# Weight splits issued one group of products earlier, and two edits in the first tile, in an attention and channel-mixing kernel

## The chip, the core and the metric

The kernel runs on one core of a Trainium2 chip. The metric is device time of the core in microseconds (us), the median of several runs. Five engines run at once, each with its own queue of instructions in order: PE (TensorE, matrix products), DVE (VectorE), ACT (ScalarE), POOL (GpSimd) and SP (SyncE, which issues most of the DMAs). An instruction of one engine that needs another's result waits in its queue, and all that stands behind it waits too.

## What is computed

Reference, cut to what matters (8 batches, 8 heads, 576 tokens, head size 64, 32 packed tokens, model width 512):

```
p_packed = softmax_attention(p, k, v)                    # 32 queries over 576 keys
attn     = softmax_attention(q, p_packed, p_packed)      # 576 queries over 32 keys
x  = attn as (batch, 576, 512)
u  = x + real(fft(fft(x, axis=tokens), axis=channels))
un = (u - mean(u)) / sqrt(var(u) + 1e-6)                 # over the 512 channels
out = u + relu(un @ w_ch1) @ w_ch2                       # w_ch1 512x2048, w_ch2 2048x512
```

## The kernel before

The 4608 tokens of the output form 36 blocks of 128, and four blocks form a tile: nine tiles, called 0 to 8 here. For each tile `ffn` (L650) runs the two layers of the channel mixing over 16 chunks `j` of 128 hidden units. A product in full precision is made of three products of rounded parts, high by high, high by low and low by high, so every operand is split into a high and a low part: `split` (L96) is a copy on ACT (L97, the high part) and a subtraction (L98, the low part), on POOL where it is told so.

- `up(j)` (L658) makes 12 products with the four 128-column pieces of w1's chunk `j` into the PSUM bank `ph` (L669); then ACT applies relu into `hh` (L672) and DVE makes the low part `hl` (L673). `ph` is one bank in all tiles but the last two, so `up(j+1)` can't start before `hl` of `j` has read it.
- `down(j)` (L676) makes 12 products of `hh`, `hl` with w2's chunk `j` into four banks `acc` (L683). It is issued one chunk late: the order on PE is `up(j)`, `down(j-1)`, `up(j+1)`, `down(j)`.
- The weights are split anew in every tile: `wsplits` (L640) is a generator that splits one chunk of w1 or w2 at each `next(splits)`, in the order w1 0, w1 1, w2 0, w1 2, w2 1, w1 3 and so on. The parts `wr_h` and `wr_l` live in a ring of six buffers, three chunks. A chunk's split takes the place of the chunk three earlier: that of w1 `j+1` waits until `down(j-2)` is over, that of w2 `j` until `up(j)` is.
- `step(i)` (L763) is called twice for each `j` (32 steps a tile): after `up(j)` and after `down(j-1)`. It issues one stage of `front(t+1)` (L235), the attention and the spectrum of the next batch, whose stages `ORDER` (L40) lists; steps 0 and 2 issue what is left of the batch before.

Stages of the front that are spoken of: scores of the packed queries and their exponentials (L263, L288), their transposes (L297, L300), the second scores (L263, `s2T`, with `s2Tt` in the bank `ph`), their transposes on DVE (L368), subtraction of maximum, mean and division (L374 to L419), the transpose to `a` (L421), `folded` (L424: sums and differences of token pairs, L431 to L436), `folded_rest` (L439: ten small ones, L449 to L462), `folded_parts` (L468: `fh`, `xl`, `ol`, `fl`), and the blocks of the result `u` (L554 to L578). `EF` (L32) says by batch and group of heads which engine folds: 0 is DVE, 1 is POOL.

In tile 0 the weights also come in. They arrive as 64-bit floats; a chunk is fetched by SP (`fetch`, L145), ACT makes two halves of it (`halves_of`, L167 and L168) and DVE joins these to the 32-bit chunk that stays in SBUF (`joined`, L172). `step(i)` of tile 0 joins a chunk, fetches the chunk three later into the place that this frees (three places, two of them tagged `wst`, one in `ubuf`), issues the front's stage and then halves the next chunk.

Inside a tile the order on PE, DVE, ACT and POOL is the order of the code (`manual_schedule`, L782). Ahead of tile 0, and where tile 0 begins, a scheduler sets the order.

Of the kernel before, what the change touches and what calls it, by code (L numbers as in the profile page):

```python
# [28 lines left out]
EN = ((0, 1), (1, 0), (0, 0))  # L29


EF = (((0, 0, 0, 0), (1, 1, 0, 0)), ((1, 1, 1, 1), (0, 0, 0, 0)), ((0, 0, 0, 0), (0, 0, 0, 0)))  # L32
ES = (1, 0, 0)
EO = (0, 0, 0)

# [40 lines left out]
def tile_kernel(ctx, tc, kpT, qT, v, w1, w2, tabs, tabR, tabB, tabT, sel, ident_d, out):  # L76
# [68 lines left out]
    def fetch(j, n):  # L145
        i = stages.pop(0)
        if i is None:
            st = work.tile([P, 512, 2], I32, tag="wst", name="wst", bufs=2)
        elif i < 0:
            st = spot(n, i, [P, 512, 2]).bitcast(I32)  # L150
        else:
            st = ubuf[:, i:i + 2, :].rearrange("p a n -> p (a n)").bitcast(I32).rearrange("p (n t) -> p n t", t=2)
        nc.sync.dma_start(st, (w1, w2)[n][:, j, :].bitcast(I32).rearrange("p (n t) -> p n t", t=2))
        fetched[j, n] = st
# [8 lines left out]
    def halves_of(j, n):  # L163

        st, high, c = words(j, n)
        fifth = st.rearrange("p n t -> p (n t)").bitcast(U8).rearrange("p (n t) -> p n t", t=8)[:, :, 3]
        nc.scalar.activation(c.bitcast(F32), high.bitcast(F32), AF.Prelu, scale=REBIAS, alpha=SIGN)  # L167
        nc.scalar.activation(high, fifth, AF.Copy, scale=1.0 / 32, bias=-31.0 / 64)  # L168

    def joined(j, n):  # L170
        st, high, c = words(j, n)
        nc.vector.scalar_tensor_tensor(c, c, 3, high, ALU.logical_shift_left, ALU.bitwise_or)  # L172
        del fetched[j, n]
# [25 lines left out]
    def next_step():  # L199
        steps[0] = (steps[0] or 0) + 1  # L200
        for item in [x for x in due if x[0] <= steps[0]]:
            due.remove(item)
            item[1]()
# [31 lines left out]
    def front(b):  # L235
# [188 lines left out]
        def folded(g):  # L424
# [4 lines left out]
            ec, oc = eo[:, 0, :], eo[:, 1, :]  # L429
            e1, e2, e3, e4 = [(nc.vector, nc.gpsimd)[i] for i in EF[min(b, 2)][g]]  # L430
            e1.tensor_tensor(ec[:, 0:287], a[:, 0:287], a[:, NE:S], ALU.add)  # L431
# [208 lines left out]
    def wsplits():  # L640

        for _ in tiles:
            for n, j in [(0, 0)] + [x for j in range(1, NJ) for x in ((0, j), (1, j - 1))] + [(1, NJ - 1)]:
                hi = work.tile([P, DM], F32R, tag="wr", name="wr_h", bufs=6)
                lo = work.tile([P, DM], F32R, tag="wr", name="wr_l", bufs=6)
                split(hi, lo, (w1f, w2f)[n][:, j, :], nc.gpsimd)
                ready.append((hi, lo))
                yield

    def ffn(first, turned, step, nxt, alone, following):  # L650
        keys = turned.keys
        n = len(keys)
        T = n * P
        uh, ul = turned.hl
        acc = [psf.tile([P, DM], F32, tag=f"acc{i}", name=f"acc{i}") for i in range(n)]
        now["acc"] = acc

        def up(j):  # L658
            wh, wl = ready.pop(0)

            pool, tag = (ps, "ps") if alone and j % 2 else (psf, "ph")
            ph = pool.tile([P, 512], F32, tag=tag, name="ph")

            step = T // 2 if first == 0 and j < SPL else T
            order = sorted(range(12), key=lambda k: k % 3 == 1) if j == 0 else range(12)
            for t in (slice(i, i + step) for i in range(0, T, step)):
                for n, k in enumerate(order):
                    c, (l, r) = k // 3, ((wh, uh), (wh, ul), (wl, uh))[k % 3]
                    nc.tensor.matmul(ph[:, t], l[:, c * P:(c + 1) * P], r[:, c, t], start=(n == 0), stop=(n == 11))  # L669
            hh = work.tile([P, 512], F32R, tag="hh", name="hh")  # L670
            hl = work.tile([P, 512], F32R, tag="hl", name="hl")
            nc.scalar.activation(hh[:, :T], ph[:, :T], AF.Relu)  # L672
            nc.vector.scalar_tensor_tensor(hl[:, :T], ph[:, :T], 0.0, hh[:, :T].bitcast(F32), ALU.max, ALU.subtract)  # L673
            return hh, hl

        def down(j, hh, hl, moves=()):  # L676

            moves = list(moves)
            vh, vl = ready.pop(0)
            for i in range(n):  # L680
                w = slice(i * P, (i + 1) * P)
                for k, (l, r) in enumerate(((hh, vh), (hh, vl), (hl, vh))):
                    nc.tensor.matmul(acc[i], l[:, w], r, start=(j == 0 and k == 0), stop=(j == NJ - 1 and k == 2))  # L683
                    if moves:
                        moves.pop(0)()

        kinds = [nxt.kind(h, following) for h in range(2)] if nxt else []
        assert kinds in ([], ["new", "late"], ["old", "new"], ["old", "old"]), kinds

        prev = None  # L690
        late = "late" in kinds
        for j in range(NJ):
            last = nxt is not None and j == NJ - 1
            cur = up(j)
            next(splits, None)
            if last:
                next(splits, None)
                nxt.parts(0)
                nxt.parts(1)
            step(2 * j)  # L700
            if j == 11:
                for h in range(2):
                    if kinds[h:h + 1] == ["old"]:
                        nxt.less_quarters(h)
                        nxt.turn(h)
            if prev is not None:
                down(j - 1, *prev, nxt.moves(2) + [lambda: None] * 4 + nxt.moves(3) if last and late else ())
                if j == 13:
                    for h in range(2):
                        if kinds[h:h + 1] == ["new"]:  # L710
                            nxt.less_quarters(h)
                if last:
                    nxt.parts(2)
                    nxt.parts(3)
                else:
                    next(splits, None)
                if late and j == NJ - 2:
                    nxt.less(2, True)
                    nxt.less(3, True)
            step(2 * j + 1)  # L720
            if j == 13:
                for h in range(2):
                    if kinds[h:h + 1] == ["new"]:
                        nxt.turn(h)
            prev = cur
        down(NJ - 1, *prev)
        next(splits, None)
        for i, key in enumerate(keys):
            u = u_of[key]
            nc.vector.scalar_tensor_tensor(u, acc[i], stat_of[key][:, 2:3], u, ALU.mult, ALU.add)  # L730
            nc.sync.dma_start(out[(first + i) * P:(first + i + 1) * P, :], u)
            free.append(place_of[key])
# [19 lines left out]
    rest = gen0  # L752
    for j in range(ORDER[0].count("D"), LEAD):
        load_weights(j)
    ready, splits = [], wsplits()
    next(splits)
    next(splits)
    for t, (first, tk) in enumerate(tiles):

        gen = front(t + 1) if t + 1 < B else iter(())  # L760
        ended = []

        def step(i):  # L763

            next_step()

            k = i + 2 * LEAD
            if t == 0 and i > 0 and k <= 2 * NJ:
                joined((k - 1) // 2, (k - 1) % 2)
                if 8 < k + 2 < 2 * NJ:  # L770
                    fetch((k + 2) // 2, (k + 2) % 2)
            if i in (0, 2):
                next(rest, None)
            elif not ended and next(gen, None) == "rest":
                ended.append(gen)
            if t == 0 and k < 2 * NJ:
                halves_of(k // 2, k % 2)
            assert i < 2 * NJ - 1 or t + 1 >= B or ended

        nxt = Turned(tiles[t + 1][1]) if t + 1 < len(tiles) else None  # L780

        with tc.manual_schedule(engines=MANUAL):  # L782
            ffn(first, cur, step, nxt, t + 1 >= B, t + 1)
        cur, rest = nxt, gen
# [112 lines left out]
```

## Time and profile before

| | us |
|---|---|
| median of 3 runs | 1008.71 (1008.37 to 1009.35) |
| the profiled execution | 1006.72 |
| its span, first to last instruction | 1004.90 |
| PE busy in the span | 953.4 (95%) |
| DVE, ACT, POOL busy | 585.5, 463.1, 477.4 |

The span falls in three: the front of batch 0 until 61 us, where PE mostly waits; tile 0 from 61 to 184 us; and eight more tiles of 91 to 107 us each. A row with a number in square brackets tells how long its engine stood idle before it, and what ended that wait.

### The profile page before, as it was taken

The page shows a single profiled execution, that of the slowest core. Times are in us where ns is not written, and L with a number is a line of the kernel's source. Part 1 is how long each engine was busy: PE and PEld are TensorE (multiplying, and loading weights), DVE is VectorE, ACT ScalarE, POOL GpSimd, SP SyncE. Part 2 cuts the span into 40 slices and gives each one's busy share as a digit, 9 for nine tenths or more (in the row PEclk, how much of TensorE's full clock was granted, in tenths as well). Part 3 has the DMA queues.
Part 4 walks back from the last instruction along what each step waited for, and adds up shares of the span by engine and source line. Part 5 has one row for each costly group of instructions (what it writes and reads, how often), then busy time and mean ns, then how long its engine had stood idle before and what let it go on. Part 6 is the DMA issues. An engine that isn't in the chain of part 4 may idle for free.

```text
span 1004.9 us, 14998 instructions
## 1 busy us (share of the span) xinstructions
PE 953.4 (95%) x5588; PEld 782.7 (78%) x5588; DVE 585.5 (58%) x1221; ACT 463.1 (46%) x942; POOL 477.4 (48%) x426
## 2 busy tenths in 40 slices
PE   4188999999999999999999999999999999999998
PEld 2176778778887888788877888788878888888886
DVE  4767795559455855578466946595658562123112
ACT  4456775544453445435544445444534453343322
POOL 3714663364345444454455434643555354545443
PEclk9599999999999999999999999999999999999999
DMA  9216442320042002300240013101410010011001
GB/s 359 110 47 201 147 147 78 130 73 0 2 133 81 0 2 73 115 1 10 58 167 1 1 56 132 48 1 47 141 48 1 22 64 1 1 28 57 0 1 42
DMA packets 28169, 65.93 MB, mean 66 GB/s; under 512 B 5494, under 2 KB 12992, under 8 KB 28096
## 3 DMA queue, kind: packets, MB, share of 16 engines
q1 hardware_dynamic: 27120, 63.53, 19.3%
q0 software_dynamic: 976, 1.44, 0.5%
q8 instruction: 44, 0.72, 0.3%
q14 instruction: 29, 0.24, 0.1%
HBM read 48.70 MB, written 9.44 MB: 58 GB/s over the span
## 4 chain that ended last, share of the span: by engine, by line
PE 79%; DVE 8%; issue 5%; POOL 4%; ACT 3%; DMA 0%; POOLq 0%; DVEq 0%; ACTq 0%
PE ph L669 34%; PE acc L683 32%; POOL wr_l L98 2%; DVE turned L413 1%; DVE turned L409 1%; PE po L320 1%; DVE w2f L172 1%; PE s L263 1%; PE px L231 1%; PE py L231 1%; PE px L233 1%; PE px L232 1%; PE py L232 1%; PE py L233 1%; ACT hh L672 1%
## 5 line engine op out<-in xcount | busy, mean ns | idle before, releaser
L98 POOL TENSOR_TENSOR wr_l<-w1f,wr_h 128x512 fp32r<-128x512 f32 x144 | 192.8, 1339 | 367.6 <-ACT wr_h L97 367.3
L673 DVE SCALAR_TENSOR_TENSOR hl<-ph,hh 128x512 fp32r<-128x512 f32 x144 | 98.9, 687 | 322.5 <-ACT hh L672 322.0
L98 POOL TENSOR_TENSOR wr_l<-w2f,wr_h 128x512 fp32r<-128x512 f32 x144 | 196.4, 1364 | 90.5 <-ACT wr_h L97 88.4
L669 PE MATMUL ph<-uh,wr_h 128*128 128x512 f32 (+1 forms) x580 | 228.4, 394 | 4.1 <-DVE s L368 2.5
L683 PE MATMUL acc<-wr_l,hh 128*128 128x512 f32 x576 | 226.5, 393 | 2.6 <-POOL wr_l L98 2.5
L669 PE MATMUL ph<-uh,wr_l 128*128 128x512 f32 (+1 forms) x580 | 225.7, 390 | 1.7 <-POOL wr_l L98 1.7
L683 PE MATMUL acc<-wr_h,hh 128*128 128x512 f32 x576 | 226.6, 393 | 0.0
L683 PE MATMUL acc<-wr_h,hl 128*128 128x512 f32 x576 | 225.8, 392 | 0.0
L672 ACT ACTIVATE hh<-ph 128x512 fp32r<-128x512 f32 x144 | 86.1, 598 | 295.3 <-PE ph L669 295.1
L669 PE MATMUL ph<-ul,wr_h 128*128 128x512 f32 (+1 forms) x580 | 220.5, 389 | 1.1 <-DVE stat L207 1.1
L669 PEld LDWEIGHTS ph<-uh,wr_h 128*128 128x128 f32 x580 | 109.1, 188 | 37.8 <-issue 8.1
L669 PEld LDWEIGHTS ph<-uh,wr_l 128*128 128x128 f32 x580 | 109.0, 188 | 25.7 <-POOL wr_l L98 2.5
L683 PEld LDWEIGHTS acc<-wr_l,hh 128*128 128x128 f32 x576 | 108.4, 188 | 26.1 <-POOL wr_l L98 4.7
L683 PEld LDWEIGHTS acc<-wr_h,hl 128*128 128x128 f32 x576 | 108.4, 188 | 23.0
L669 PEld LDWEIGHTS ph<-ul,wr_h 128*128 128x128 f32 x580 | 108.8, 188 | 22.2 <-DVE stat L207 1.3
L683 PEld LDWEIGHTS acc<-wr_h,hh 128*128 128x128 f32 x576 | 108.3, 188 | 22.2
L97 ACT CAST wr_h<-w2f 128x512 fp32r<-128x512 f32 x144 | 88.9, 617 | 0.0
L97 ACT CAST wr_h<-w1f 128x512 fp32r<-128x512 f32 x144 | 88.3, 613 | 0.0
L231 PE MATMUL py<-gh,fh 128*128 128x258 f32 x64 | 19.3, 301 | 26.8 <-ACT fh L473 26.8
L211 ACT ACTIVATE junk<-ubuf,stat 128x512 f32<-128x512 f32 x36 | 25.7, 716 | 27.1 <-DVE stat L207 27.1
L98 POOL TENSOR_TENSOR gl<-turned,gh 128x516 fp32r<-128x516 f32 x16 | 24.9, 1555 | 24.6 <-ACT gh L97 24.6
L231 PEld LDWEIGHTS py<-gh,fh 128*128 128x128 f32 x64 | 12.9, 202 | 27.9 <-ACT fh L473 27.4
(202 smaller groups left out, 1299.4 us busy)
## 6 DMA issues: line engine op xcount, KB each, us to landing
kp<-kpT SPq DMA_DIRECT2D x16, 608.0 KB, 3.9
out<-ubuf SPq DMA_DIRECT2D x36, 256.0 KB, 2.1
vt<-v SPq DMA_DIRECT2D x14, 640.0 KB, 5.0
wst<-w SPq DMA_DIRECT2D x17, 512.0 KB, 3.6
qt<-qT SPq DMA_DIRECT2D x14, 576.0 KB, 4.4
raw<-flip SPq DMA_DIRECT2D x208, 32.0 KB, 1.8
ubuf<-w SPq DMA_DIRECT2D x9, 512.0 KB, 3.7
w1f<-w SPq DMA_DIRECT2D x3, 512.0 KB, 13.6
```

The source lines that it names most:

```text
L97: nc.scalar.copy(hi, src)
L98: (lo_eng or nc.vector).tensor_tensor(lo, src, hi.bitcast(F32), ALU.subtract)
L172: nc.vector.scalar_tensor_tensor(c, c, 3, high, ALU.logical_shift_left, ALU.bitwise_or)
L211: nc.scalar.activation(junk, u, AF.Square, bias=st[:, 1:2], scale=1.0, accum_out=st[:, 2:3])
L231: nc.tensor.matmul(o, lh, rh, start=first, stop=False)
L232: nc.tensor.matmul(o, lh, rl, start=False, stop=False)
L233: nc.tensor.matmul(o, ll, rh, start=False, stop=last)
L263: nc.tensor.matmul(res[g][c][at, :w.stop - w.start], lhs(g, h), rhs(g, h, w), start=True, stop=True, tile_position=(r, h * NPK))
L669: nc.tensor.matmul(ph[:, t], l[:, c * P:(c + 1) * P], r[:, c, t], start=(n == 0), stop=(n == 11))
L672: nc.scalar.activation(hh[:, :T], ph[:, :T], AF.Relu)
L673: nc.vector.scalar_tensor_tensor(hl[:, :T], ph[:, :T], 0.0, hh[:, :T].bitcast(F32), ALU.max, ALU.subtract)
L683: nc.tensor.matmul(acc[i], l[:, w], r, start=(j == 0 and k == 0), stop=(j == NJ - 1 and k == 2))
```

## The change

Three edits. In `up(j)` the split of the next w1 chunk is issued right behind the products, ahead of relu, and not behind it; the split of w2 `j` is issued right behind relu and `hl`, ahead of `step(2j)` and of `down(j-1)`, and not behind both. `EF` now gives the folds of batch 1, group 0, to DVE; these are issued in tile 0. In `step` of tile 0 the joining and the fetch stand behind the front's stage and no longer ahead of it.

```diff
-EF = (((0, 0, 0, 0), (1, 1, 0, 0)), ((1, 1, 1, 1), (0, 0, 0, 0)), ((0, 0, 0, 0), (0, 0, 0, 0)))
+EF = (((0, 0, 0, 0), (1, 1, 0, 0)), ((0, 0, 0, 0), (0, 0, 0, 0)), ((0, 0, 0, 0), (0, 0, 0, 0)))
...
                     nc.tensor.matmul(ph[:, t], l[:, c * P:(c + 1) * P], r[:, c, t], start=(n == 0), stop=(n == 11))
+            next(splits, None)
             hh = work.tile([P, 512], F32R, tag="hh", name="hh")
...
             cur = up(j)
-            next(splits, None)
+            if prev is not None:
+                next(splits, None)
             if last:
-                next(splits, None)
                 nxt.parts(0)
...
                     nxt.parts(3)
-                else:
-                    next(splits, None)
                 if late and j == NJ - 2:
...
+        next(splits, None)
         down(NJ - 1, *prev)
-        next(splits, None)
...
             k = i + 2 * LEAD
+            if i in (0, 2):
+                next(rest, None)
+            elif not ended and next(gen, None) == "rest":
+                ended.append(gen)
             if t == 0 and i > 0 and k <= 2 * NJ:
                 joined((k - 1) // 2, (k - 1) % 2)
                 if 8 < k + 2 < 2 * NJ:
                     fetch((k + 2) // 2, (k + 2) % 2)
-            if i in (0, 2):
-                next(rest, None)
-            elif not ended and next(gen, None) == "rest":
-                ended.append(gen)
             if t == 0 and k < 2 * NJ:
```

What stands where, at three places. First POOL in the front of batch 0, ahead of tile 0: L391 and L419 are the subtraction of the mean and the division for group 1, `wr_l` the low parts of weights. Before:

```order
L98 TENSOR_TENSOR gl<-turned,gh 128x516
L98 TENSOR_TENSOR wr_l<-w1f,wr_h 128x512 x2
L391 TENSOR_TENSOR s_276<-s_276,d_338 128x576
L419 TENSOR_TENSOR s_276<-s_276,z_337 128x576
L449 TENSOR_TENSOR f<-a 128x3 x2
```

Now:

```order
L98 TENSOR_TENSOR gl<-turned,gh 128x516
L98 TENSOR_TENSOR wr_l<-w1f,wr_h 128x512 x2
L391 TENSOR_TENSOR s_276<-s_276,d_338 128x576
L98 TENSOR_TENSOR wr_l<-w2f,wr_h 128x512
L419 TENSOR_TENSOR s_276<-s_276,z_337 128x576
L449 TENSOR_TENSOR f<-a 128x3 x2
```

The third split, that of w2 0, which stood behind tile 0's first relu, now stands between L391 and L419.

Second ACT in tile 0, from relu of chunk 5 on (L378 and L379 are exponentials of the front). Before:

```order
L672 ACTIVATE hh<-ph 128x512
L97 CAST wr_h<-w1f 128x512
L378 ACTIVATE s_1031<-s_1031 128x576
L379 ACTIVATE s_1031<-s_1031 128x576
L167 ACTIVATE w1f<-wst 128x512
L168 ACTIVATE wst<-wst 128x512
L97 CAST wr_h<-w2f 128x512
L378 ACTIVATE s_1032<-s_1032 128x576
L379 ACTIVATE s_1032<-s_1032 128x576
L167 ACTIVATE w2f<-wst 128x512
L168 ACTIVATE wst<-wst 128x512
L672 ACTIVATE hh<-ph 128x512
```

Now:

```order
L97 CAST wr_h<-w1f 128x512
L673 ACTIVATE hh<-ph 128x512
L97 CAST wr_h<-w2f 128x512
L378 ACTIVATE s_1029<-s_1029 128x576
L379 ACTIVATE s_1029<-s_1029 128x576
L167 ACTIVATE w1f<-wst 128x512
L168 ACTIVATE wst<-wst 128x512
L378 ACTIVATE s_1030<-s_1030 128x576
L379 ACTIVATE s_1030<-s_1030 128x576
L167 ACTIVATE w2f<-wst 128x512
L168 ACTIVATE wst<-wst 128x512
L97 CAST wr_h<-w1f 128x512
```

The copy of w1 6 has moved from behind relu of chunk 5 to ahead of it, and that of w2 5 from behind a pair of exponentials and a pair of halves to right behind that relu; in tiles 1 to 8 the two copies and relu stand the same way, without L167 and L168.

Third DVE in tile 0, from `hl` of chunk 1 on (L575 to L578 make the last block of batch 0; `e1tq` is the bank that PE fills with transposes next). Before:

```order
L673 SCALAR_TENSOR_TENSOR hl<-ph,hh 128x512
L172 SCALAR_TENSOR_TENSOR w2f<-w2f,wst 128x512
L575 TENSOR_TENSOR xa<-px,spec_682 64x512
L577 TENSOR_TENSOR ubuf<-xa,spec_692 64x256
L578 TENSOR_TENSOR ubuf<-xa,spec_692 64x256
```

Now:

```order
L674 SCALAR_TENSOR_TENSOR hl<-ph,hh 128x512
L575 TENSOR_TENSOR xa<-px,spec_682 64x512
L577 TENSOR_TENSOR ubuf<-xa,spec_692 64x256
L578 TENSOR_TENSOR ubuf<-xa,spec_692 64x256
L172 SCALAR_TENSOR_TENSOR w2f<-w2f,wst 128x512
```

The joining has moved behind the front's three instructions, as in every step of tile 0; on SP the fetch that follows a joining moves with it, so that the second load of queries (`qt`) now stands ahead of two `wst` fetches where it stood between them.

## Rows read from the trace of the kernel before

**Rows 1.** Windows: us; busy us (count) PE, PEld, DVE, ACT, POOL; PEclk, DMA, GB/s.

```profile
61.00:184.10 123.10, 113.03 (x673) 90.64 (x674) 84.61 (x174) 82.92 (x160) 60.95 (x53) 0.99 0.43 132
184.10:291.40 107.30, 106.97 (x654) 88.26 (x653) 70.07 (x152) 49.80 (x104) 51.28 (x45) 1.00 0.16 52
...
102.40:142.80 40.40, 36.31 (x145) 27.55 (x144) 31.93 (x60) 29.35 (x52) 27.64 (x22) 0.96 0.52 157
```

**Rows 2.** Timeline of PE in tile 0: start, duration, instruction, [idle before <-releaser].

```profile
79.54 0.41 PE L300 MATMUL e1tq<-ident,e 128*64 128x128 f32 x2 [2.14 <-DVE xa L575]
...
94.60 0.28 PE L263 MATMUL s2Tt<-qt,ppT 64*32 64x64 f32 x7 [0.76 <-DMA qt<-qT]
...
96.35 0.47 PE L669 MATMUL ph<-uh,wr_h 128*128 128x512 f32 x1 [0.55 <-DVE s L368]
...
107.87 0.40 PE L669 MATMUL ph<-uh,wr_h 128*128 128x512 f32 x1
108.11 0.40 PE L669 MATMUL ph<-ul,wr_h 128*128 128x512 f32 x1
109.36 0.50 PE L669 MATMUL ph<-uh,wr_l 128*128 128x512 f32 x1 [0.85 <-POOL wr_l L98]
...
171.34 0.39 PE L231 MATMUL px<-bdh,oh 128*128 128x256 f32 x1 [0.75 <-ACT spec L531]
```

**Rows 3.** Timeline of POOL and PE in the front of batch 0.

```profile
35.30 1.53 POOL L391 TENSOR_TENSOR s<-s,d 128x576 f32<-128x576 f32 x1
37.84 1.41 POOL L419 TENSOR_TENSOR s<-s,z 128x576 f32<-128x576 f32 x1 [1.00 <-DVE z L390]
...
40.14 0.68 POOL L449 TENSOR_TENSOR f<-a 128x3 f32<-128x3 f32 x2 [0.89 <-DVE a L421]
...
45.75 0.58 PE L231 MATMUL py<-gh,fh 128*128 128x258 f32 x1 [26.34 <-ACT fh L473]
```

**Rows 4.** Timeline of DVE, POOL and SP in tile 0.

```profile
77.12 1.77 DVE L172 SCALAR_TENSOR_TENSOR w2f<-w2f,wst 128x512 int32<-128x512 int32 x1
...
77.06 1.27 POOL L98 TENSOR_TENSOR wr_l<-w1f,wr_h 128x512 fp32r<-128x512 f32 x1 [7.25 <-ACT wr_h L97]
...
87.74 0.38 SPq L227 DMA_DIRECT2D qt<-qT  x1
```

**Rows 5.** Groups by line, 98.6 to 145.6: count, busy us, mean ns, idle.

```profile
L431 POOL TENSOR_TENSOR eo<-a 128x287 f32<-128x287 f32 x1 | 1.1, 1147 | 0.0
L433 POOL TENSOR_TENSOR f<-eo 128x128 f32<-128x128 f32 x1 | 0.5, 464 | 0.0
...
L172 DVE SCALAR_TENSOR_TENSOR w1f<-w1f,wst 128x512 int32<-128x512 int32 x5 | 3.9, 783 | 0.4 <-ACT wst L168 0.4
...
L431 DVE TENSOR_TENSOR eo<-a 128x287 f32<-128x287 f32 x1 | 0.4, 446 | 0.0
L433 DVE TENSOR_TENSOR f<-eo 128x128 f32<-128x128 f32 x1 | 0.3, 277 | 0.0
...
L168 ACT ACTIVATE wst<-wst 128x512 int32<-128x512 uint8 x9 | 6.1, 677 | 0.3
```

**Rows 6.** DMA issues: count, KB each, us from issue to landing.

```profile
wst<-w SPq DMA_DIRECT2D x17, 512.0 KB, 3.6
```

**Rows 7.** Timeline of DVE, PE and ACT in tile 2.

```profile
317.56 1.82 DVE L413 TENSOR_TENSOR turned<-turned 128x258 f32<-128x258 f32 x2
...
319.68 0.47 PE L669 MATMUL ph<-uh,wr_h 128*128 128x512 f32 x1 [0.33 <-DVE s L368]
...
339.58 0.60 ACT L672 ACTIVATE hh<-ph 128x512 fp32r<-128x512 f32 x1 [3.81 <-PE ph L669]
340.08 0.61 ACT L97 CAST wr_h<-w1f 128x512 fp32r<-128x512 f32 x1
...
357.04 0.67 DVE L673 SCALAR_TENSOR_TENSOR hl<-ph,hh 128x512 fp32r<-128x512 f32 x1
...
358.42 0.39 PE L669 MATMUL ph<-uh,wr_h 128*128 128x512 f32 x1
```

## The prediction

> **What bounds the kernel now.** I read the windows first. In tile 1 PE is busy 106.97 of 107.30 us at the full granted clock (1.00) [rows 1]; five of the tiles behind it show the same 0.32 to 0.33 us of idle time. There the kernel is as fast as its products, and no earlier split can gain more than that third of a microsecond a tile. Tile 0 is 123.10 us long and PE busy 113.03 of it [rows 1]: 10.1 us of idle time, and the rest of the difference is work that no other tile has, and a lower clock. So the change is worth what it does in tile 0, plus 0.33 us in each of six tiles, less what it adds to the front.
>
> Second I read PE's timeline in tile 0 for the brackets [rows 2]. The reader is to see three kinds of waits: one of 2.14 us behind DVE (`xa`), a pair of 0.76 and 0.55 us at the second scores, and waits for POOL's `wr_l`, of which 0.85 us at 109.36 is one; there are five between 109 and 141 us. Third, the window that holds those five: 102.40 to 142.80, from the start of `up(5)` to that of `up(11)`, is 40.40 us with PE busy 36.31 and a mean clock of 0.96 [rows 1].
>
> **The change part by part.** All times are made against the profiled execution, 1006.72 us, which lies 2.0 us below the median of the runs, 1008.71; the sum is carried to the median by that difference.
>
> 1. *The split that went into the front.* POOL's third `wr_l` now stands between L391 and L419. Before, L391 ended at 36.83 (35.30 and 1.53), and L419 began at 37.84, a microsecond later, released by DVE's L390 [rows 3]. L419 leads to the transpose to `a`, this to POOL's L449 at 40.14 ("DVE a L421"), and POOL's small folds to `fh`, for which PE waits 26.34 us [rows 3]: a chain with no other slack. A `wr_l` takes 1.27 us [rows 4], so it fills the microsecond and adds 0.3; L390 and a joining beside it may be held up too, as far as L419's own 1.41 shows, 1.1 in all. I take +0.8, nearer the upper end, since L390 falls into the inserted instruction. No gain is possible here. ACT's copy for it falls into idle time.
>
> 2. *DVE's joined chunk behind the front, at `e1tq`.* PE waited 2.14 us for `xa`; ahead of `xa` stood a joining of 1.77 us at 77.12 [rows 2, 4]. It now follows. The reductions of the scores also come ahead of a joining, so ACT's exponentials, and relu behind them, start earlier. Of 2.14 at least 1.2 goes; I take all, −2.1, because both causes act.
>
> 3. *Queries.* The second load of queries was issued at 87.74 [rows 4], behind a fetch that waited for its place. It now stands ahead of that fetch, and can go when the buffer is free, 3 us sooner. That removes the 0.76; the 0.55 behind it waits for DVE's L368, which two joinings no longer precede. −1.3, with 0 as the other end: the place may be limited by the values' buffer.
>
> 4. *The stretch from `up(5)` to `up(11)`.* PE's idle time is 40.40 less 36.31, 4.1 us; the clock of 0.96 costs 40.40 by 0.04, 1.6 us, a piece at the lower of the clock's two levels, 1.2 in place of 2.4 GHz, that follows PE's longest stop there. Each of the five stops costs more than its bracket: the product at 109.36 started 1.25 us after the one at 108.11, where that one had followed 0.24 after the product before it, so 1.0 is lost and 0.85 listed, and the next product 0.1 more [rows 2]; 0.28 by five is 1.4 us. Together 7.1 us can be had. With the new order the `wr_l` waits go: a w1 chunk's copy (0.61 [rows 7]) and `wr_l` (1.27 [rows 4]) stand in the time of `up(j)`, one group of products before `down(j-1)`, and w2's follow relu, with two groups until they are needed.
> What is late next is `hl`. ACT is loaded in each of these chunks by relu, two copies, two pairs of halves (0.68 and the same once more each [rows 5]) and the front, some 5.2 of the 5.4 us that two groups, 24 products some 0.23 apart, take. The fetch now leaves behind the front's instructions on DVE, 3.6 us later it lands [rows 6], and ACT, in order, stops at a half whose chunk is still on the way, with a copy and relu behind it. I followed the new order by hand from `up(5)` on, each instruction as long as in these rows and not before what it needs. At chunk 9: PE wants `ph` for `up(10)` 5.4 us after the start of `up(9)`. ACT gets to chunk 23's half at 2.6 (behind `xh` and `oh`, which wait for DVE's folds), is through with the pair at 3.9, the copy at 4.4, relu at 4.9; DVE's `hl` stands behind a joining which POOL's `wr_l` may hold up, and ends between 6.2 and 7.0. PE waits about 1.4. At `up(8)`, `up(9)` and `up(11)` the same way gives 0.2, 0.5 and 0.4. That is 2.5 given back, and −4.6 net; the ends are −7.1 with nothing given back and 0 with all.
>
> 5. *The folds.* POOL's two at 1147 ns and four at 464 become two at 446 and four at 277 on DVE [rows 5] (L431 and L433 stand for their likes): POOL is freed of 4.1 us, DVE takes 2.0. It is inside part 4: the folds stood ahead of the `wr_l` that PE waited longest for.
>
> 6. *Spectrum copy.* PE waits 0.75 for ACT's `spec` at 171.34 [rows 2]. The chain to it ran through a joining on DVE that now follows the front. −0.8; 0 as the other end.
>
> 7. *Tiles 1 to 6.* The 0.33 at 319.68 ends with L368, behind L413, whose two took 1.82 us [rows 7] because a `wr_l` ran beside them. In the new order both `wr_l` of that time are over by then. Six by 0.33 is −2.0; 0 as the other end, and by the same row no more than 0.33 can be lost for this cause again. One more `wr_l` wait of 0.2 goes near the end: −0.2.
>
> Sum: 0.8 − 2.1 − 1.3 − 4.6 − 0.8 − 2.0 − 0.2 = −10.2 us. 1006.72 − 10.2 = 996.5; with the 2.0 us to the median, **998.5**.
>
> **The rivals.**
>
> *VectorE and GpSimd share what they read SBUF through.* The joining at 77.12 took 1.77 us where the group's mean is 783 ns; POOL's `wr_l` ran from 77.06 to 78.33, and the joining ended 0.56 later [rows 4, 5]: it stood still meanwhile. If this sharing sets the pace of part 4's stretch, moving splits about in it brings nothing, and it shrinks only by the folds, 4.1 − 2.0 = 2.1 in place of 4.6: 998.5 + 2.5 = **1001.0**. For it: POOL is busy 27.64 and DVE 31.93 of 40.40 [rows 1]. Against it: DVE's reductions and `hl` don't stand still, and both engines idle there. The Trainium skill, "SBUF — State Buffer", section "SBUF: two separate sides", has the pair as an exclusive lock, held for a whole instruction; the rows agree, and the rule gives this rival's time.
>
> *The ring of three places.* A joining frees the place for a fetch: 3.6 to land, 1.35 for halves, then relu and a copy, 1.2, `hl` and the front's instructions on DVE, about 3. That is 9.2 for three steps, and where the front's chain through POOL delays a joining more, 10.1; twelve steps would take 40.4, as long as before, and part 4 gives nothing: 998.5 + 4.6 = **1003.1**. Against it: before, ACT met only landed chunks.
>
> *Slower: relu behind the copy in all tiles.* `ph` is a single bank. If the copy ahead of relu waits (for its buffer, or ACT is late), relu and `hl` come up to 0.61 + 1.27 = 1.9 us later. At chunk 10 of tile 2 `hl` ends at 357.71 and `up(11)` starts at 358.42 [rows 7]: past 0.71 us PE waits. 1.2 lost in three chunks of six tiles would be 22 us: **1020**. Against it: relu at 339.58 ended an idle time of 3.81 us on ACT [rows 7], and the buffer is free when `up(j)` starts, so the copy fits ahead.
>
> *It does little.* The copies wait in ACT's queue as long as before, and only part 1 is left: **1009.5**.
>
> **How the numbers follow.** The forecast, 995 to 1001: 0.58; better than that 0.03; the shared port 0.16; the ring 0.11; little 0.05; slower 0.07. The bounds of the parts: everything at its good end is −10.2 − 2.5 − 0.5, 995.5 for the median; the port together with no gain in parts 3 and 7 is 1004.3. Range 995.0 to 1004.5; it leaves out 0.15 to 0.2. This kernel's measurement tells 0.2%, 2.0 us, from no change. Faster by more: 0.58 + 0.03 + 0.16 + 0.11 and a little less for a ring that also costs part 3, 0.86. Within: 0.07. Slower: 0.07.
>
> **What would show it.** Right: PE's first `ph` product of tile 0 about 0.8 later; no stop at `e1tq` nor for `qt`; `up(5)` to `up(11)` in 35 to 37 us with no wait for `wr_l` and short ones for `hl`; full clock in that stretch; tiles 1 to 6 without the 0.33; tile 0 in 113 to 115 us. The port shows as the stretch at 38 us with DVE's joinings at 1.8; the ring as idle ACT ahead of L167, ended by a DMA; the slower case as PE waiting for `hl` in tiles 1 to 6. The prediction is wrong if tile 0's gain is given back in `ph` waits of more than 5 us, or if a wait turns up in the later tiles.

## The result and the profile after

The changed kernel takes 996.06 us in the median (995.06 to 998.08, five runs), a ratio of 0.9876 to before (95% interval 0.9861 to 0.9890): 12.65 us faster, where 10.2 were forecast. The profiled execution took 998.08 us with a span of 996.3; it is the longest of the five (the other spans are 993.3 to 994.7), while the one profiled before lay 2.0 us below its median. So the two traces differ by 8.6 us only, and this has to be kept apart from what the change does.

Windows of the changed kernel over the same pieces of the program as [rows 1], tile 0, tile 1, and `up(5)` to `up(11)` (us; busy us and count of PE, PEld, DVE, ACT, POOL; clock, DMA, GB/s):

```profile
62.75:178.45 115.70, 111.12 (x672) 90.62 (x673) 79.55 (x181) 83.24 (x159) 54.89 (x47) 0.99 0.45 142
178.45:285.35 106.90, 106.90 (x653) 88.26 (x652) 65.57 (x152) 50.22 (x104) 52.62 (x44) 1.00 0.16 51
101.65:138.10 36.45, 33.81 (x145) 26.45 (x143) 31.06 (x62) 28.25 (x50) 21.35 (x15) 1.00 0.53 160
```

Tile 0 went from 123.10 to 115.70 us, the stretch from 40.40 to 36.45 and back to the full clock, and in tile 1 PE has no idle time left. PE's waits from 95 to 147 us (engine, line, releaser: us in all, times, longest), the rows on `wr_l` of before, then all rows of after:

```profile
PE acc L683 <- POOL wr_l L98: 2.3, 3, 1.9
PE ph L669 <- POOL wr_l L98: 1.7, 2, 0.9
```

```profile
PE ph L669 <- DVE hl L674: 2.7, 3, 1.2
PE ph L669 <- DVE s L368: 0.2, 1, 0.2
```

Every wait for `wr_l` is gone. The three for `hl` that came in their place stand in PE's timeline, as do the places of [rows 2] where PE waited for `xa` and `qt` (no bracket now):

```profile
80.29 0.38 PE L300 MATMUL e1tq<-ident,e 128*64 128x128 f32 x2
...
94.20 0.34 PE L263 MATMUL s2Tt<-qt,ppT 64*32 64x64 f32 x16
...
95.57 0.47 PE L669 MATMUL ph<-uh,wr_h 128*128 128x512 f32 x1 [0.16 <-DVE s L368]
...
119.33 0.50 PE L669 MATMUL ph<-uh,wr_h 128*128 128x512 f32 x1 [1.01 <-DVE hl L674]
...
125.52 0.50 PE L669 MATMUL ph<-uh,wr_h 128*128 128x512 f32 x1 [0.45 <-DVE hl L674]
...
138.12 0.50 PE L669 MATMUL ph<-uh,wr_h 128*128 128x512 f32 x1 [1.21 <-DVE hl L674]
```

The product at [rows 7], behind the second scores of tile 2, follows them without a bracket (313.27 us); from 190 us to the end the changed kernel's trace lists no wait of PE at all.

**All kernels by stage.** Each column is a difference of start times in the profiled execution of that kernel: from L391 on POOL in the front to PE's first product with `fh` (F); from the first product of `up(0)` to `up(1)` of tile 0; then to `up(5)`, to `up(11)`, to tile 1, and through tiles 1 to 7. The label of a kernel is that of its experiment, below. Each ratio is to executions of before made beside that kernel, whose medians lie between 1007.76 and 1008.71; so kernels are compared by their ratios, and a median alone can be off by up to 1 us.

| kernel | median us | ratio, 95% interval | F | 0 to 1 | 1 to 5 | 5 to 11 | 11 to tile 1 | tiles 1-7 |
|---|---|---|---|---|---|---|---|---|
| before | 1008.71 | | 10.45 | 9.07 | 32.37 | 40.42 | 41.24 | 729.68 |
| after | 996.06 | 0.9876 (0.9861-0.9890) | 10.85 | 10.32 | 28.58 | 36.44 | 40.35 | 726.72 |
| splits_alone | 1004.63 | 0.9965 (0.9953-0.9977) | 10.86 | 9.07 | 31.39 | 41.96 | 40.84 | 726.81 |
| folds_alone | 1007.14 | 0.9988 (0.9979-0.9997) | 10.45 | 9.05 | 33.88 | 38.78 | 41.34 | 729.55 |
| order_alone | 1004.20 | 0.9955 (0.9943-0.9968) | 10.45 | 10.33 | 28.42 | 40.74 | 40.21 | 729.92 |
| no_splits | 1002.27 | 0.9951 (0.9938-0.9964) | 10.45 | 11.75 | 28.36 | 38.82 | 41.69 | 729.53 |
| no_folds | 996.71 | 0.9895 (0.9880-0.9911) | 10.83 | 9.07 | 28.58 | 36.75 | 40.44 | 726.72 |
| no_order | 1004.93 | 0.9974 (0.9966-0.9983) | 10.84 | 9.08 | 31.33 | 41.94 | 40.85 | 726.82 |
| third_back | 995.40 | 0.9874 (0.9861-0.9887) | 10.45 | 9.08 | 28.61 | 36.56 | 40.34 | 726.72 |
| ring6 | 996.86 | 0.9890 (0.9876-0.9904) | 10.83 | 10.33 | 28.73 | 35.60 | 40.36 | 726.72 |
| ring6_even | 995.88 | 0.9871 (0.9855-0.9888) | 10.82 | 9.06 | 29.19 | 37.34 | 40.23 | 726.85 |
| ring6_steps | 996.02 | 0.9877 (0.9862-0.9891) | 10.86 | 9.04 | 28.56 | 36.43 | 40.34 | 726.72 |
| combined | 995.32 | 0.9869 (0.9855-0.9884) | 10.45 | 9.05 | 29.40 | 36.90 | 40.21 | 726.73 |
| ring6_no_low | 992.86 | 0.9844 (0.9830-0.9858) | 10.82 | 9.05 | 28.53 | 33.09 | 40.21 | 726.72 |

### The profile page after: what moved, and what is told of

Its sections match the earlier page's. It is cut to its first block, busy times and chain, and to the rows that moved or that the text cites. A ratio compares the mean times of both kernels' runs of the same rounds, so it can differ in the third digit from the quotient of the medians.

```text
span 996.3 us, 15070 instructions
## 1 busy us (share of the span) xinstructions
PE 953.2 (96%) x5588; PEld 784.4 (79%) x5588; DVE 552.2 (55%) x1227; ACT 469.9 (47%) x942; POOL 477.1 (48%) x420
## 4 chain that ended last, share of the span: by engine, by line
PE 91%; DVE 4%; ACT 2%; POOL 1%; DMA 1%; issue 1%; DVEq 0%; POOLq 0%; ACTq 0%
PE ph L669 38%; PE acc L684 38%; PE po L320 1%; PE s L263 1%; PE px L233 1%; PE px L232 1%; PE px L231 1%; PE py L231 1%; PE e1tp L297 1%; PE py L232 1%; PE py L233 1%; PE pz L231 1%; PE pz L233 1%; PE pz L232 1%; PE s2T L263 1%
## 5 line engine op out<-in xcount | busy, mean ns | idle before, releaser
L98 POOL TENSOR_TENSOR wr_l<-w1f,wr_h 128x512 fp32r<-128x512 f32 x144 | 199.5, 1386 | 280.7 <-ACT wr_h L97 228.6
L98 POOL TENSOR_TENSOR wr_l<-w2f,wr_h 128x512 fp32r<-128x512 f32 x144 | 190.3, 1322 | 160.1 <-ACT wr_h L97 153.2
L215 POOL TENSOR_TENSOR stat<-stat,mhalf 128x1 f32<-128x1 f32 x36 | 23.6, 671 | 25.6 <-DVE stat L214 25.6
```

Source lines behind the costliest of these rows:

```text
L98: (lo_eng or nc.vector).tensor_tensor(lo, src, hi.bitcast(F32), ALU.subtract)
L215: nc.gpsimd.tensor_tensor(st[:, 2:3], st[:, 2:3], mhalf, ALU.pow)
```

## The experiments

### The three edits, one at a time

Each is the kernel before with one edit of the change. splits_alone:

```diff
+            next(splits, None)
             hh = work.tile([P, 512], F32R, tag="hh", name="hh")
...
-            next(splits, None)
+            if prev is not None:
+                next(splits, None)
             if last:
-                next(splits, None)
...
-                else:
-                    next(splits, None)
...
+        next(splits, None)
         down(NJ - 1, *prev)
-        next(splits, None)
```

> Before, with the splits moved and nothing else. The forecast's parts 4 and 7: the waits for `wr_l` go in every tile, the third split lies in the front, the joined chunks still stand ahead of the front on DVE and the first tile's folds on POOL, so the stops of 2.1 us for `xa`, 0.76 for `qt` and 0.75 for `spec` stay. About -0.4 us for each of tiles 1 to 7 (-2.8), -2 to -3 in the stretch from up(5) to up(11), +0.4 in the front: 1003.5 to 1004.5 us against 1008.7. If VectorE's and GpSimd's sharing sets the pace of the stretch, it brings nothing there: 1006.3. If copies wait in ScalarE's queue as before: 1008.7 or more.

folds_alone:

```diff
-EF = (((0, 0, 0, 0), (1, 1, 0, 0)), ((1, 1, 1, 1), (0, 0, 0, 0)), ((0, 0, 0, 0), (0, 0, 0, 0)))
+EF = (((0, 0, 0, 0), (1, 1, 0, 0)), ((0, 0, 0, 0), (0, 0, 0, 0)), ((0, 0, 0, 0), (0, 0, 0, 0)))
```

> Before, with the first tile's folds on VectorE and nothing else. POOL is freed of 4.1 us ahead of the `wr_l` that PE waited longest for (2.05 us at up(10)) and of one more of 0.4; with the piece at the lower clock behind that stop gone too: -2.4 to -4 us, 1005 to 1006.3. By the shared port: -2.1, 1006.6. If another `wr_l` or `hl` takes the place of that wait: 1008.7.

order_alone:

```diff
+            if i in (0, 2):
+                next(rest, None)
+            elif not ended and next(gen, None) == "rest":
+                ended.append(gen)
             if t == 0 and i > 0 and k <= 2 * NJ:
                 joined((k - 1) // 2, (k - 1) % 2)
...
-            if i in (0, 2):
-                next(rest, None)
-            elif not ended and next(gen, None) == "rest":
-                ended.append(gen)
```

> Before, with the joined chunks and fetches of the first tile behind the front's step and nothing else. Parts 2, 3 and 6: the stops for `xa` (2.1), `qt` (1.3 with what follows it) and `spec` (0.8) go: -4.2 us, 1004.5. Tiles 1 to 7 keep their 0.33 to 0.47 each. If the ring of three places paces the first tile, a later fetch costs in the stretch what is won ahead of it: 1007 to 1008.7.

The medians of the first and the third came close to what was expected: 1004.6 and 1004.2. But the splits won in another place than was thought. Tiles 1 to 7 gained 2.9 us, as expected, and `up(1)` to `up(5)` 1.0; the stretch, for which 2 to 3 us less were expected, became 1.5 us longer. The stops that were to stay did so in part only: PE's wait for `xa` is 1.7 us for 2.1, that for `spec` 0.2 for 0.8, and that for `qt` is gone. PE's waits from 95 to 147 us (splits_alone):

```profile
PE ph L669 <- DVE hl L674: 6.2, 4, 2.8
PE ph L669 <- DVE s L368: 0.6, 1, 0.6
```

All waits for `wr_l` went, 4.0 us, and 6.2 for `hl` came. The longest, 2.8, is seen in DVE's and POOL's timelines of the same kernel:

```profile
125.83 1.79 DVE L172 SCALAR_TENSOR_TENSOR w1f<-w1f,wst 128x512 int32<-128x512 int32 x1
127.55 1.86 DVE L419 TENSOR_TENSOR s<-s,z 128x576 f32<-128x576 f32 x1
129.44 0.78 DVE L421 STREAM_TRANSPOSE a<-s 128x576 f32<-128x576 f32 x1
130.15 0.65 DVE L674 SCALAR_TENSOR_TENSOR hl<-ph,hh 128x512 fp32r<-128x512 f32 x1
...
125.42 1.66 POOL L98 TENSOR_TENSOR wr_l<-w1f,wr_h 128x512 fp32r<-128x512 f32 x1 [2.05 <-ACT wr_h L97]
127.04 1.76 POOL L98 TENSOR_TENSOR wr_l<-w2f,wr_h 128x512 fp32r<-128x512 f32 x1
```

The two `wr_l` of a chunk now come one behind the other. DVE's joining takes 1.79 us beside the first (0.68 where POOL is still), its product L419 takes 1.86 beside the second (0.75), and `hl`, whose relu had begun at 125.35, stands behind both until 130.15. The Trainium skill, "SBUF — State Buffer", section "SBUF: two separate sides", has the pair of ports that the two engines share as an exclusive lock held for a whole instruction; these rows agree, with 1.1 us lost at each.

`folds_alone` gained 0.1% (expected 0.24 to 0.37%). The stretch is 1.6 us shorter, but hardly by its waits: PE stands idle there for 3.9 us (38.78 less 34.90 busy) where it stood for 4.1. The wait of 1.9 us for `wr_l` is gone, and others have come, one of 1.1 for `hl` among them. What the stretch gained is the clock, 1.00 in place of 0.96; the piece at half the clock lies earlier in this trace, from 79.42 to 82.83 us, behind the stop for `xa`, where `up(1)` to `up(5)` takes 33.88 for 32.37.

`order_alone` took out the stops for `xa`, `qt` and `spec`: 3.95 us in `up(1)` to `up(5)` and 1.0 behind `up(11)`. The stretch is about as long as before (40.74 for 40.42), so beside the waits for `wr_l` that are still there the ring of three places costs 0.3 us at most.

### The change less one edit

The changed kernel, with one of the three diffs above taken back.

> The changed kernel with the splits where they were before: folds on VectorE and the joined chunks behind the front stay. If the edits add up: 1008.7 - 4.2 for the order - 2.4 for the folds = 1002 us. If the waits for `wr_l` in the stretch come from POOL's folds alone, only tiles 1 to 7 (2.9 us) and the front's 0.4 are given up against the changed kernel: 998.6.

> The changed kernel with the first tile's folds on GpSimd, as before. If the sooner splits leave POOL enough time, the folds' 4.1 us are hidden there: 996 to 996.5 us. If the folds still stand ahead of a `wr_l` that PE needs, or hold ScalarE's halves behind `xh`: 998 to 999, with a wait for POOL or `fh` in up(9) to up(11).

> The changed kernel with the joined chunks and fetches ahead of the front's step, as before. The stops for `xa`, `qt` and `spec` come back: +4.2 us, 1000.3. In the stretch from up(5) to up(11) the fetches leave sooner: if the waits for `hl` there (3.2 us) come from chunks that land late, some of them go and the kernel is at 998 to 999.

Without the splits the kernel is 0.49% faster than before; the two others alone add up to 0.57%. Without the folds it can't be told from the changed kernel: 996.7, and 0.3 us more in the stretch. So the folds are worth next to nothing, by themselves or beside the two others. Without the order it is at 1004.9, worse than the 1000.3 expected, and no better than the splits alone; its stretch has the same waits, 6.2 us for `hl`.

The order and the splits belong together. Apart they are worth 0.45% and 0.35%, together (no_folds) 1.05%; the rest, 0.25% or 2.5 us, comes only when both are there (the three intervals together leave some 0.2% of doubt on it). In the stretch it is plain: +1.5 for the splits, +0.3 for the order, −3.7 for both. In PE's idle time alone it is +2.2, +0.3 and −1.2 from 4.1; most of what the −3.7 has beyond that is the clock, 0.96 in the stretch of before, splits_alone and order_alone, 1.00 with both. With the order L419 and the joining ahead of that `hl` took 0.75 and 0.65 us, at a time without `wr_l` (DVE, changed kernel):

```profile
121.79 0.75 DVE L419 TENSOR_TENSOR s<-s,z 128x576 f32<-128x576 f32 x1
...
123.27 0.65 DVE L172 SCALAR_TENSOR_TENSOR w1f<-w1f,wst 128x512 int32<-128x512 int32 x1
124.77 0.69 DVE L674 SCALAR_TENSOR_TENSOR hl<-ph,hh 128x512 fp32r<-128x512 f32 x1 [0.85 <-ACT hh L673]
```

That it is this shift and not another one of the same edit is read from the rows, no run separates it.

### The third split and the front

```diff
-            next(splits, None)
+            if first or j:
+                next(splits, None)
...
-            if prev is not None:
+            if prev is not None or not first:
                 next(splits, None)
```

> The changed kernel with the first w2 chunk's split issued behind the first relu of tile 0, as before, and so out of the front on POOL and ScalarE. Between L391 and L419 on POOL the trace of the changed kernel shows 2.71 us against 2.54 before, and L419 itself 0.2 longer: by that the third split costs 0.4 us, and without it 995.7 us. If all of the 1.8 us by which tile 0's first product came later is the split's: 994.3. If down(0) or the second scores then wait for this split: 996 to 997.5.

The median is 995.4, which the intervals don't tell from 996.06. The trace does tell: the column F is 10.45 us in all six kernels that have no third split in the front, and 10.82 to 10.86 in all eight that have it. It costs 0.4 us. POOL in the front, changed kernel, against [rows 3]:

```profile
36.04 1.53 POOL L391 TENSOR_TENSOR s<-s,d 128x576 f32<-128x576 f32 x1
37.53 1.30 POOL L98 TENSOR_TENSOR wr_l<-w2f,wr_h 128x512 fp32r<-128x512 f32 x1
38.75 1.64 POOL L419 TENSOR_TENSOR s<-s,z 128x576 f32<-128x576 f32 x1
```

L419 starts 2.71 us behind L391 where it was 2.54, and takes 1.64 for 1.41. Its first row also shows what is not the edit's: L391 itself is 0.74 us later (36.04 for 35.30), with nothing changed ahead of it. Over all fourteen traces L391 starts between 34.66 and 36.29, in no relation to the edits: no_folds, whose front is that of the changed kernel, has 34.66.

The other part of tile 0's late start is the clock. Two windows of the changed kernel, and the same two of before:

```profile
61.00:64.86 3.86, 2.17 (x16) 1.72 (x15) 3.86 (x13) 2.09 (x6) 1.10 (x2) 1.00 0.00 0
64.86:68.28 3.42, 2.93 (x12) 2.53 (x12) 1.70 (x7) 2.00 (x6) 1.24 (x2) 0.50 0.00 0
```

```profile
61.00:64.86 3.86, 2.80 (x20) 2.37 (x20) 3.27 (x12) 1.91 (x5) 1.25 (x3) 1.00 0.00 0
64.86:68.28 3.42, 2.69 (x23) 2.68 (x23) 1.60 (x3) 1.63 (x4) 0.18 (x1) 1.00 0.00 0
```

In the trace of after the clock is at its lower level, 1.2 GHz, for 3.42 us; `up(0)` to `up(1)` takes 10.32 in place of 9.07. In ten of the fourteen traces this piece is 9.04 to 9.08, with the edits and without; 10.32 or 10.33 in three, 11.75 in one. third_back and no_folds, each one edit away from the changed kernel, have 9.08 and 9.07. So the edits don't make the 1.25 us. Whether the other four executions of the changed kernel had such a piece no trace shows; their mean clocks, 0.982 to 0.984 beside 0.983 of the profiled one, don't say that they were without.

### What is left in the stretch

Of the 36.44 us some 33 are products; the waits for `hl` take the rest. The prediction had put them down to ACT, which stops at a half whose chunk is still on its way. ACT's waits for DMAs in the changed kernel, 100 to 140 us:

```profile
ACT w1f L167 <- DMA wst<-w: 2.6, 1, 2.6
ACT w1f L167 <- DMA ubuf<-w: 1.7, 2, 1.2
ACT w2f L167 <- DMA ubuf<-w: 1.5, 1, 1.5
ACT w2f L167 <- DMA wst<-w: 1.0, 1, 1.0
```

That is 6.8 us, so a kernel with more places tells what they cost:

```diff
-STG1 = [9, None, None]
+STG1 = [9, None, None, -2, -2, -4] * 3 + [9, None, None, -2, 9, None, None, 9]
...
+    for k in (9, 10, 11):
+        fetch(k // 2, k % 2)
...
-                if 8 < k + 2 < 2 * NJ:
-                    fetch((k + 2) // 2, (k + 2) % 2)
+                m = k + 5 if k <= 22 else {25: 28, 26: 29, 27: 30, 29: 31}.get(k)
+                if m:
+                    fetch(m // 2, m % 2)
```

> The changed kernel with six places for chunks on their way in place of three: the parts of w1f and w2f that hold chunks 12 to 15 later serve as three more, so a fetch leaves three steps sooner. If the waits for `hl` that are left in up(8) to up(11) (1.17, 0.61 and 1.37 us in the trace) come from halves that stand behind a chunk still on its way, they go: 993 to 993.5 us, and ScalarE shows no idle time ahead of L167 that a DMA ended. If ScalarE's work itself or VectorE behind POOL sets them: 995.5 to 996.5.

All of ACT's waits for DMAs in the stretch went, and the stretch fell by 0.84 us only; the median didn't move. Two waits for `hl` of about 1 us are left, at `up(8)` and `up(9)`. Relu is on time there, `hl` isn't (ACT, then DVE, ring6):

```profile
115.79 0.60 ACT L673 ACTIVATE hh<-ph 128x512 fp32r<-128x512 f32 x1 [0.28 <-PE ph L669]
...
117.04 0.78 DVE L421 STREAM_TRANSPOSE a<-s 128x576 f32<-128x576 f32 x1 [1.05 <-POOL s L419]
117.75 1.08 DVE L172 SCALAR_TENSOR_TENSOR w1f<-w1f,ubuf 128x512 int32<-128x512 int32 x1
118.75 0.68 DVE L674 SCALAR_TENSOR_TENSOR hl<-ph,hh 128x512 fp32r<-128x512 f32 x1
...
120.12 1.24 DVE L388 TENSOR_SCALAR d<-z 128x18 f32<-128x18 f32 x1
...
124.48 1.09 DVE L172 SCALAR_TENSOR_TENSOR w1f<-w1f,wst 128x512 int32<-128x512 int32 x1
125.50 0.68 DVE L674 SCALAR_TENSOR_TENSOR hl<-ph,hh 128x512 fp32r<-128x512 f32 x1
```

So what is left of the wait is in DVE's queue. Three kernels changed what stands in it:

ring6_even, on top of ring6:

```diff
-            if t == 0 and i > 0 and k <= 2 * NJ:
-                joined((k - 1) // 2, (k - 1) % 2)
-                m = k + 5 if k <= 22 else {25: 28, 26: 29, 27: 30, 29: 31}.get(k)
+            for x in (i - 1, i) if t == 0 and 0 < i < 28 and i % 2 == 0 else ():
+                x += 5
+                joined(x // 2, x % 2)
+                m = x + 6 if x < 22 else {24: 28, 25: 29, 26: 30, 28: 31}.get(x)
```

> The kernel with six places, with both joined chunks of a chunk pair in the even steps, right behind `hl`, and none in the odd ones, where one stood ahead of the next `hl`. If what is left of the waits for `hl` (1.1 us each at up(8) and up(9) with six places) is the joining of 1.08 us that stands still beside a `wr_l` ahead of `hl` on VectorE: 0.5 to 1.1 less at each, the stretch from up(5) to up(11) at 33.5 to 34.5 us in place of 35.6, some 995 us. If it is the transpose to `a` that waits for GpSimd: the stretch stays at 35 to 36.

ring6_steps, on top of ring6:

```diff
-EN = ((0, 1), (1, 0), (0, 0))
+EN = ((0, 1), (0, 0), (0, 0))
```

> The kernel with six places, with the three steps of the weights (L375, L391, L419) of tile 0's first group on VectorE in place of GpSimd. If `hl` of chunk 7 comes late since the transpose ahead of it waits for GpSimd's L419 (118.75, with relu at 115.79), its wait of 1.1 us at up(8) goes, while VectorE takes three more instructions of about 0.7 us: the stretch at 34.5 us. If VectorE's work paces there: 36 or more.

combined has this diff, that of ring6_even and that of third_back on top of ring6's.

> Six places, the joined chunks in the even steps, the three steps on VectorE and the first w2 chunk's split out of the front, all together. If each removes its own wait: the stretch from up(5) to up(11) at 33 to 33.5 us (PE is busy 32.6 to 33 there at the full clock), the front 0.4 shorter, 993 us in the median, 3 below the changed kernel. If one wait takes the place of another: 994.5 to 996.

None did what was hoped. With the even steps the two waits at `up(8)` and `up(9)` fall to one of 0.4, and one of 1.8 comes at `up(10)`, with 3.41 us at the lower clock behind it: 37.34. With L375, L391 and L419 on DVE the wait at `up(8)` grows to 1.5: 36.43. Combined, 36.90, and a median of 995.3 that the intervals don't tell from the changed kernel; one stop of 1.8 is left, and behind it the clock is at 0.50 from 130.11 to 133.53, where products are 0.43 us apart in place of 0.23: some 1.6 us lost there by itself (an estimate). The stop at `up(10)` of the combined kernel (DVE, then POOL, then PE):

```profile
125.39 1.35 DVE L449 TENSOR_TENSOR f<-a 128x3 f32<-128x3 f32 x2
126.65 1.26 DVE L457 COPY f<-eo 128x3 f32<-128x3 f32 x1
...
128.09 0.68 DVE L674 SCALAR_TENSOR_TENSOR hl<-ph,hh 128x512 fp32r<-128x512 f32 x1
...
125.29 1.35 POOL L98 TENSOR_TENSOR wr_l<-w1f,wr_h 128x512 fp32r<-128x512 f32 x1 [2.98 <-ACT wr_h L97]
126.60 1.28 POOL L98 TENSOR_TENSOR wr_l<-w2f,wr_h 128x512 fp32r<-128x512 f32 x1
...
128.82 0.50 PE L669 MATMUL ph<-uh,wr_h 128*128 128x512 f32 x1 [1.77 <-DVE hl L674]
```

Instructions on three columns, 0.22 and 0.15 us where POOL is still, take 1.35 and 1.26: each stands until a `wr_l` is over. In these three kernels it didn't matter much what stood ahead of `hl`: while two `wr_l` ran, DVE didn't get through it. The last kernel leaves `wr_l` out in tile 0, from chunk 2 on, on top of ring6; products that would read it read `wr_h` again, so their number stays and the low parts are missing from the result. It is a kernel to measure with, not to use:

```diff
+                if tile == 0 and j > 1:
+                    nc.scalar.copy(hi, (w1f, w2f)[n][:, j, :])
+                    ready.append((hi, hi))
+                    yield
+                    continue
                 lo = work.tile([P, DM], F32R, tag="wr", name="wr_l", bufs=6)
```

> The kernel with six places, without the low parts of tile 0's weights from chunk 2 on: GpSimd's `wr_l` are left out there and the products that would read them read `wr_h` in their place, so TensorE has as many products of the same size. What VectorE and ScalarE issue stays the same. If VectorE's instructions that stand still beside `wr_l` (6.8 us in the stretch from up(5) to up(11) with six places) are what makes `hl` late there: no wait for `hl` is left, the stretch at 33 to 33.5 us in place of 35.6, some 993 to 994 us. If VectorE's own work or the hand-over to GpSimd's L419 makes it late: two waits of about 1 us stay, 35 to 35.6.

The windows of the stretch in ring6 and in ring6_no_low:

```profile
101.83:137.44 35.61, 33.59 (x146) 26.62 (x144) 31.11 (x62) 28.13 (x50) 21.19 (x15) 1.00 0.45 134
```

```profile
100.09:133.18 33.09, 33.09 (x146) 26.87 (x144) 27.22 (x74) 29.33 (x52) 5.55 (x4) 1.00 0.51 153
```

PE doesn't wait any more, and DVE is through 74 instructions in 27.22 us where it had 62 in 31.11. The rows that answer to those of ring6 (DVE, ring6_no_low):

```profile
114.72 0.78 DVE L421 STREAM_TRANSPOSE a<-s 128x576 f32<-128x576 f32 x1 [1.06 <-POOL s L419]
115.42 0.65 DVE L172 SCALAR_TENSOR_TENSOR w1f<-w1f,ubuf 128x512 int32<-128x512 int32 x1
115.99 0.68 DVE L679 SCALAR_TENSOR_TENSOR hl<-ph,hh 128x512 fp32r<-128x512 f32 x1
...
117.37 0.18 DVE L388 TENSOR_SCALAR d<-z 128x18 f32<-128x18 f32 x1
...
120.67 0.65 DVE L172 SCALAR_TENSOR_TENSOR w1f<-w1f,wst 128x512 int32<-128x512 int32 x1
121.24 0.68 DVE L679 SCALAR_TENSOR_TENSOR hl<-ph,hh 128x512 fp32r<-128x512 f32 x1
```

Counted from the start of `up(8)` (119.48 and 116.73), that chunk's `hl` starts after 6.02 us with `wr_l` and 4.51 without. The 1.5 between are L388, 1.24 for 0.18, and the joining, 1.09 for 0.65. For the chunk before (`up(7)` at 112.74 and 110.99) it is 6.01 and 5.00: 0.43 is the joining, the rest that GpSimd's own steps come sooner when no `wr_l` stands ahead of them in its queue. So of the 3.4 us that the changed kernel's stretch has above 33.1, taken away in this order, 0.8 are chunks that land late and 2.5 are `wr_l`; by the rows of these two chunks mostly by holding DVE up, partly by its place in POOL's queue. A chunk without `wr_l` also takes one buffer of the weights' ring and not two, which no run separates; but at these two chunks of ring6 relu, which follows the copies on ACT, wasn't late. The ratio fell from 0.9890 to 0.9844, more than the stretch's 2.5 us: the trace of ring6 has the low piece in `up(0)` to `up(1)` besides, 10.33 for 9.05.

## Why the prediction was right, and where not

The direction and most of the size were right, and the reason for the gain, waits of tile 0 and a third of a microsecond in the later tiles, too. Two of the signs named ahead missed: PE's first product of tile 0 came 1.8 us later, not 0.8, and tile 0 took 115.7 us, not 113 to 115. By its parts, from the traces:

| part | forecast | measured |
|---|---|---|
| 1 third split in the front | +0.8 | +0.4 |
| 2, 3 `xa` and queries (`up(1)` to `up(5)`) | −3.4 | −3.8 |
| 4, 5 stretch | −4.6 | −4.0 |
| 6 spectrum copy | −0.8 | −0.9 |
| 7 tiles 1 to 7 | −2.2 | −3.0 |
| sum | −10.2 | −11.3 |
| start of tile 0, not made by the edits | 0 | +2.6 |
| traces | −10.2 | −8.6 |

- **Part 1** was half its size. L419 was not held up by all of 1.1 us; it took 0.2 longer, and the added 1.30 nearly fitted the idle microsecond.
- **Parts 2, 3 and 6** are right: the brackets went as forecast, and a little more; that for `qt` goes with the splits alone, too.
- **Part 4** was right in size, wrong in two reasons. The net of 4.6 was 4.0, the stretch 36.4 in the forecast's 35 to 37, and the clock was full; 1.4 of the 4.0 is idle time of PE (4.1 to 2.7), 2.6 less busy time, most of it the low piece that is gone. But the waits for `hl` came at `up(8)`, `up(9)` and `up(11)` with 1.2, 0.6 and 1.4 us of lost time, 3.2 in all, where the working by hand had 0.2, 0.5, 1.4 at `up(10)` and 0.4, 2.5 in all. It followed ACT's queue closely and DVE's by the usual durations. Landing chunks are 0.8 of what is left, `wr_l` 2.5. And the gain was put down to the splits; by themselves they make the stretch longer (41.96).
- **Part 5** said that POOL's folds stood ahead of the longest wait for `wr_l`. True of the kernel before: in folds_alone that wait went. But the stretch's idle time fell by 0.2 us only, and with splits and order in place the folds are worth 0.3.
- **Part 7** was too small by 0.8: tiles 1 to 6 gained 0.38 to 0.47 each for a bracket of 0.33, and tile 7 0.51; a stop costs more than its bracket. Part 4 had counted that, 0.28 a stop; part 7 hadn't.
- **The way to the median** failed. The 2.0 us between the profiled execution of before and its median were added to the forecast, as if they belonged to every execution of the changed kernel. Tile 0's late start shows what such a difference is made of: 0.7 from the front ahead of the edits, 0.6 from the first low piece of the clock, which lasted until 54.62 us in place of 52.02, and 1.25 from the second. For before the record says more. Of 48 executions timed beside the experiments, 12 had the mean granted clock of the profiled one, 0.983, and a median of 1006.5 us; the 36 others, at 0.979 to 0.982, had 1008.5. So the profiled execution was one of the less frequent kind, and the 2.0 us go with the clock: 0.002 of 1005 us is 2.0 (an estimate). The traces' sum of the change itself, −11.3, is 1.3 short of the medians' −12.65; where in the span the untraced executions had the lower clock, and how much of it the changed kernel has, stays open.

**The rivals.** The shared port as the pace of the stretch, 38 us, didn't come: 36.4. But its mechanism is what most of the remaining wait is made of, and in the kernel with the splits alone it makes the longest stop. The chance of 0.16 was for a rival that is half true. The ring of three fell: six places win 0.8 us in the stretch and nothing that the median shows. The slower case fell: PE has no wait for `hl` in tiles 1 to 6. That it does little fell with the first table.

## What to carry to other kernels

When an instruction is issued sooner, look not only at who waits for it but at what it will run beside: the splits cured all waits for `wr_l` in tile 0, and without the second edit gave more than that back; by the rows of the longest stop, because two `wr_l` in a row held VectorE's queue ahead of `hl`. And look at the clock of a stretch before its length is put down to waits: a piece at the lower level that moved to another stretch made the folds look 1.4 us better than they were. Edits that feed one queue are to be priced together, and a stop that is removed is worth its bracket and the refill behind it. A forecast made against one profiled execution should carry its distance to the median as uncertainty, not as a constant.

## What was not expected of the hardware

- Some VectorE instructions, however small, stand until GpSimd's is over: one on 128x3 elements took 1.26 us beside a `wr_l` of 1.28, and 0.15 otherwise; one on 128x18 took 1.24 for 0.18. Others run on: `hl`, which reads a PSUM bank, took 0.68 beside a `wr_l` (118.75 in ring6, beside POOL's from 118.24 to 119.98).
- The clock fell beside stops of about 2 us. In the stretch it fell to 1.2 GHz in the six kernels in which PE stood still once for 1.77 to 2.8 us (before, splits_alone, order_alone, no_order, ring6_even, combined), within 1.4 us of that stop's end, in two of them before it; and in none of the eight others, whose longest stop is 1.5. The length of the stop doesn't decide alone: behind the same 2.14 us for `xa` the clock fell in folds_alone (79.42) and not in before. At the start of tile 0 kernels that differ there in nothing had the lower clock or not.
